# An adaLN attention and Mish MLP block on one core: the transposes of the last two blocks' normalised tiles go by 32 x 32 squares through DRAM and VectorE, and sums of weights are made at other places

## The chip, the cores and the metric

The kernel runs on one core of one Trainium2 chip. The metric is the device time in microseconds (us) of one execution. TensorE (PE) multiplies matrices out of SBUF into PSUM, VectorE (DVE), ScalarE (ACT) and GpSimd (POOL) work element by element, and SyncE (SP) and GpSimd issue most of the DMAs.

## The reference

2048 rows of 512 numbers; the MLP is 1792 wide. Everything is float32.

```
mod = (silu(c) @ w_mod).reshape(1, 6, 1, 512)
sa, ca, ga, sb, cb, gb = mod[:, 0..5]
h = layernorm(x) * (1 + ca) + sa
q, k, v = heads(h @ wqkv)                      # 32 heads of 16
phi = lambda t: where(t > 0, t + 1, exp(t)) + 1e-6
kv = einsum("bhsd,bhse->bhde", phi(k), v);  z = phi(k).sum over rows
o = einsum(phi(q), kv) / (einsum(phi(q), z) + 1e-6)
x = x + ga * (o @ wo)
h = layernorm(x) * (1 + cb) + sb
out = x + gb * (mish(h @ w1 + b1) @ w2)        # mish(t) = t * tanh(softplus(t))
```

## The kernel before

**Arithmetic.** Each operand of a matrix product is split into a high part `h` (rounded to the matmul's fp32r type, made on ScalarE or GpSimd) and a low part `l` (the rest, made on VectorE, L88 or L90). A product is three matmuls: high by high, low by high, high by low (`mm3`, lines L74 to L76 of the profile). q and the MLP use a scheme of seven products in place of eight on 2 x 2 blocks, for which sums and differences of the operands are made first: `q_left`/`q_right` for q, `rows` for w1, `columns` for the activations' side, `w2_sums` for w2, `left_sums` for its left operands.

**Blocks.** The rows are four blocks of 512, each of four tiles of 128 rows (`t`). A tile of x is normalised (`ln_side`: statistics, `ln_apply`), and the normalised tiles are needed in two layouts: as they are (`xn`, for `g_unit`, which sums k-by-x products) and turned (`hT`, for k and q). The turned tiles are made by `transpose`: sixteen 128 x 128 transposes on TensorE a block (L237) into a PSUM tile, from which ScalarE makes the scaled tile `hf` (L243), whose high and low parts are `hT`. After attention, the second normalisation makes n tiles (`norm_tile`); those of blocks 2 and 3 are stored to DRAM (`nd`), loaded back (`load_back`), and turned on TensorE by `transpose_f` (L919).

**Stages, by the profile's time.** Up to 24 us block 0 starts up; to 107 us `k_unit` and `g_unit` of blocks 1, 2, 3 alternate and end with z (the sum of phi(k), L295); to 130 us q of blocks 0 and 1 (`q_sevens`) and `kv_ps`, the product that gives kv (L968); to 157 us q of blocks 2 and 3, with m = kv by wo (`m_ps`) between; to 211 us the outputs `o_unit` and the second normalisation of blocks 0 and 1; to 312 us the MLP of these two (pairs of w1's tiles g, `pair_unit`, with `d_unit` for w2 behind); to 352 us the second half of that (`second`); to 436 us the pairs of blocks 2 and 3; to the end their sevenths with w2.

**What sets the order.** The code is in the order of execution for each engine. TensorE's work is written out; work for the other engines is in generators that are put on a list by `spawn`, and `tick()` moves each of these one step further (up to its next `yield`). A second list (`spawn_idle`) lets its first two (three in the last phase) move at each tick. So the place of a VectorE, ScalarE or DMA instruction is set by the tick in which its step falls, and an engine carries its instructions out in that order, waiting at each until its inputs are there. All tiles of 128 x 512 share one pool of 101 places.

**Weights.** `rows(g)` loads the two w1 tiles of pair g (L716), makes four sums and differences of 128 x 256 (L722 to L725) and splits them into high and low; `store_rows` writes the parts to DRAM for g below 5, and `load_rows` reads them back through GpSimd's queue (L756) for blocks 2 and 3. `w2_job(f)` scales a w2 tile by gb, splits it and stores the parts; for pairs below 5 it stores the scaled tile too (`w2f`). `w2_sums(g)` loads these (L671) or takes the tile at hand, makes four differences of 128 x 256 and splits them, and stores the result to `w2t`. `wo_scale` scales wo by ga and splits it. `z_side` makes what the denominator needs from z.

Of the kernel before, what the change touches and what calls it, by code (L numbers as in the profile page):

```python
# [13 lines left out]
P = 128  # L14
# [11 lines left out]
def block_kernel(ctx: ExitStack, tc: tile.TileContext, x, wqkv, wo, w1, b1t, w2, c, wmodt, out):  # L26
# [205 lines left out]

    def transpose(key, b, j, sc0, sh0, ptag, hi_engine=act):

        p = ps(ptag, f"tp_{key}_{b}_{j}")
        for t in range(4):
            pe.transpose(p[:, P * t:P * (t + 1)], xt[key, b, t][:, P * j:P * (j + 1)], ident)  # L237

        def post():
            hf = sb(f"hf_{key}_{b}_{j}")  # L240
            if b < 2:
                hfx[b, j] = hf
            act.activation(hf, p, AF.Identity, bias=mc[:, sh0 + j:sh0 + j + 1], scale=mc[:, sc0 + j:sc0 + j + 1])  # L243
            yield from split(f"hT_{key}_{b}_{j}", hf, hT, (key, b, j), hi_engine=hi_engine)
# [178 lines left out]
    def ln_side(b):  # L423
        for j in range(4):
            ln_stats("x", b, j, xt["x", b, j])
            if j == 3:
                ln_eps("x", b)
                ln_rstd("x", b)
            yield
        ln_shift("x", b)  # L430
# [165 lines left out]
    def wo_scale():  # L596

        for k in range(4):
            dve.tensor_tensor(wos[k], wos[k], bc["ga"], op=ALU.mult)
            yield  # L600
            yield from split(f"wos_{k}", wos[k], wos, k)
# [6 lines left out]
    def z_side():  # L608
# [7 lines left out]
        for g in range(4):  # L616
# [3 lines left out]
            dve.tensor_scalar(hmask[:, g, :], hmask[:, g, :], zc[:, g:g + 1], 1.0, op0=ALU.mult, op1=ALU.mult)  # L620
        for k in range(4):
            zs[k] = sb(f"zs_{k}")
            dve.tensor_scalar(zs[k], zbc, mc[:, k:k + 1], 1.0, op0=ALU.mult, op1=ALU.mult)

        dve.tensor_reduce(zh, zbc.rearrange("p (h r) -> p h r", r=16), op=ALU.add, axis=mybir.AxisListType.X)
# [17 lines left out]
    def w2_job(f, wait=2):  # L643
# [10 lines left out]
        if n == 0:  # L654
            w2f[g] = drp.tile([P, 2, D], F32, name=f"w2f_{g}")
# [4 lines left out]
        if g < KEPT:  # L660
            pool.dma_start(w2f[g][:, n, :], t)

    w2t, w2k, wb = {}, {}, {}
    W2_AT = {0: 6, 1: 5, 2: 0, 3: 1, 6: 2}

    def w2_sums(g):

        if g < KEPT:
# [26 lines left out]
        for i in range(2):  # L695
            for n in range(2):
                sp.dma_start(d[:, n, 2 * i:2 * i + 2, :], f32(keep[i][n]).rearrange("p (t c) -> p t c", t=2))
# [13 lines left out]
    def rows(g, wait):  # L711

        r = [sb(f"w1p_{g}_{i}", F32, (P, 4, P)) for i in range(2)]
        for i in range(2):
            f = 2 * g + i
            sp.dma_start(r[i], w1[:, P * f:P * (f + 1)].rearrange("(k p) f -> p k f", p=P))  # L716
        for _ in range(wait):
# [10 lines left out]
        op_rows[g] = keep  # L728
# [13 lines left out]
    op_rows, rows_d = {}, {}  # L742

    def store_rows(g):
# [684 lines left out]
```

## Time and profile before

| | us |
|---|---|
| median of 3 runs (lowest, highest) | 495.04 (493.94, 495.09) |
| span of the profiled execution | 493.7 |
| TensorE busy in it | 486.8 (99%) |
| VectorE busy | 370.3 (75%) |
| ScalarE busy | 298.1 (60%) |
| GpSimd busy | 144.0 (29%) |

The profiled execution's own time is its span and what lies around it; the times of the runs lie about 1.3 us above the span (495.04 to 493.7). A row of the profile names a line of the kernel, an engine, an operation and the tiles written and read, with buffer numbers left out. An engine that is idle has a releaser, the event that ended its wait.

### The profile page before, as it was taken

To read this page: it belongs to the slowest core of one execution; us is meant where nothing else is said; L and a number is where in the kernel's file an instruction comes from. 1 tells how busy PE (TensorE), PEld (TensorE's weight loads), DVE (VectorE), ACT (ScalarE), POOL (GpSimd) and SP (SyncE) were. 2 spreads that over 40 slices of the span, in tenths; PEclk is the share of its full clock that TensorE was granted. 3 is DMA by queue.
4 is the path that set the end of the run, shared out by engine and by line. 5 is a ranking of instruction groups with operands and counts; after the bars stand their busy time and mean duration, and the time that the engine had idled before them with its cause. 6 is when DMAs were issued, how large, how long until landed. Compare 5 with 4: busy or idle time off the path is not lost.

```text
span 493.7 us, 7708 instructions
## 1 busy us (share of the span) xinstructions
PE 486.8 (99%) x2638; PEld 412.0 (83%) x2638; DVE 370.3 (75%) x715; ACT 298.1 (60%) x533; POOL 144.0 (29%) x242
## 2 busy tenths in 40 slices
PE   7999999999999999999999999999999999999997
PEld 5788888878878888888888888888888888899997
DVE  6888889899799699976877563789732666769872
ACT  6886587866555879737767655288045555568100
POOL 3673111000023124103432435114644410545200
PEclk9999999999999999999999999999999999999999
DMA  8813545144873417388899979999996704688512
GB/s 303 295 43 90 163 100 118 43 132 148 285 197 108 107 54 254 117 283 304 271 327 312 308 237 280 333 289 357 387 309 193 218 23 123 179 206 229 134 44 86
DMA packets 66785, 98.58 MB, mean 200 GB/s; under 512 B 7057, under 2 KB 31641, under 8 KB 66746
## 3 DMA queue, kind: packets, MB, share of 16 engines
q1 hardware_dynamic: 37896, 53.63, 32.7%
q0 software_dynamic: 28704, 44.19, 32.5%
q8 instruction: 21, 0.34, 0.3%
q10 hardware_dynamic: 146, 0.26, 0.1%
q14 instruction: 18, 0.15, 0.1%
HBM read 62.92 MB, written 33.03 MB: 194 GB/s over the span
## 4 chain that ended last, share of the span: by engine, by line
PE 97%; DMA 1%; ACT 1%; DVE 0%; SPq 0%; issue 0%; DVEq 0%; ACTq 0%
PE p_a L1064 19%; PE p_s L1064 8%; PE oacc L76 5%; PE oacc L75 5%; PE oacc L74 5%; PE m L76 5%; PE m L75 5%; PE m L74 5%; PE o L74 3%; PE gacc L75 3%; PE gacc L76 3%; PE o L76 3%; PE gacc L74 3%; PE o L75 3%; PE pq_a L345 3%; PE pk L76 2%
## 5 line engine op out<-in xcount | busy, mean ns | idle before, releaser
L199 POOL TENSOR_TENSOR rs_n<-rs_n,half 128x1 f32<-128x1 f32 x16 | 11.4, 710 | 63.3 <-DVE rs_n L194 36.6
L1069 DVE TENSOR_TENSOR cb<-p_s,u 128x512 f32<-128x512 f32 x28 | 19.2, 687 | 13.0 <-ACT u L1105 13.0
L1099 ACT ACTIVATE u<-p_a 128x512 f32<-128x512 f32 x12 | 7.2, 598 | 29.0 <-PE p_a L1064 29.0
L1074 ACT ACTIVATE u<-p_a 128x512 f32<-128x512 f32 x14 | 8.4, 598 | 25.5 <-PE p_a L1064 25.5
L1056 ACT ACTIVATE ub<-cb,b1c 128x512 f32<-128x512 f32 x28 | 20.0, 717 | 4.9 <-DVE cb L1069 4.7
L1327 POOL DMA_DIRECT2D wt_m<-w2t x20 | 14.0, 702 | 26.8 <-DVE cb L1069 14.7
L921 ACT ACTIVATE hf_n<-tp_n,mc 128x512 f32<-128x512 f32 x16 | 11.7, 767 | 12.8 <-PE tp_n L919 12.8
L1105 ACT ACTIVATE u<-p_a 128x512 f32<-128x512 f32 x14 | 8.3, 596 | 17.0 <-PE p_a L1064 13.8
L709 POOL DMA_DIRECT2D w2b<-w2d x20 | 10.6, 532 | 24.0 <-DMA w2t<-t_5h 4.6
L259 DVE SCALAR_TENSOR_TENSOR ku<-e_k,relu_k 128x512 f32<-128x512 f32 x16 | 11.0, 688 | 7.1 <-ACT relu_k L257 7.0
L1069 DVE TENSOR_TENSOR c<-p_a,u 128x512 f32<-128x512 f32 x14 | 9.6, 689 | 8.5 <-PE p_a L1064 6.5
L256 ACT ACTIVATE e_k<-pk 128x512 f32<-128x512 f32 x16 | 9.5, 596 | 9.5 <-PE pk L76 9.5
L821 POOL DMA_DIRECT2D rden_d<-rden x2 | 1.4, 718 | 45.9 <-DVE rden L819 45.9
L703 POOL DMA_DIRECT2D wb<-w2d x14 | 9.9, 710 | 14.9 <-PE p_a L1064 12.4
L199 POOL TENSOR_TENSOR rs_x<-rs_x,half 128x1 f32<-128x1 f32 (+1 forms) x10 | 7.4, 742 | 23.3 <-DVE rs_x L194 22.5
L1033 ACT ACTIVATE u<-p_a,b1c 128x512 f32<-128x512 f32 x14 | 9.6, 687 | 6.9 <-PE p_a L1064 6.9
L259 DVE SCALAR_TENSOR_TENSOR q<-e_q,relu_q 128x512 f32<-128x512 f32 x16 | 10.7, 686 | 3.1 <-ACT relu_q L257 3.1
L208 ACT ACTIVATE x<-x,nb_x,rs_x 128x512 f32<-128x512 f32 x13 | 10.0, 808 | 4.9 <-DVE nb_x L203 3.8
L268 POOL DMA_DIRECT2D ku<-ku x8 | 7.2, 899 | 18.8 <-DVE ku L259 18.8
L845 DVE TENSOR_TENSOR r<-o,r 128x512 f32<-128x512 f32 x16 | 10.8, 677 | 1.0 <-PE o L76 0.9
L833 DVE SCALAR_TENSOR_TENSOR q<-q,rd 128x512 f32<-128x512 f32 x16 | 10.4, 685 | 1.1 <-DMA rd<-rden_d 1.1
L190 DVE BATCH_NORM_STATS2 st_x<-x 128x6 f32<-128x512 f32 x13 | 8.9, 681 | 2.9 <-DMA x<-in_x_dram 2.9
(1573 smaller groups left out, 1974.5 us busy)
## 6 DMA issues: line engine op xcount, KB each, us to landing
wm<-in_wmodt_dram SPq DMA_DIRECT2D x24, 256.0 KB, 5.8
w2b<-w2d POOLq DMA_DIRECT2D x20, 256.0 KB, 6.4
wt_m<-w2t POOLq DMA_DIRECT2D x20, 256.0 KB, 4.2
r<-in_x_dram SPq DMA_DIRECT2D x16, 256.0 KB, 2.8
x<-in_x_dram SPq DMA_DIRECT2D x15, 256.0 KB, 4.6
w1p<-in_w_dram SPq DMA_DIRECT2D x14, 256.0 KB, 5.2
w2r<-in_w_dram SPq DMA_DIRECT2D x14, 256.0 KB, 5.3
wb<-w2d POOLq DMA_DIRECT2D x14, 256.0 KB, 5.0
```

Of the source, the lines that this page charges most:

```text
L74: pe.matmul(o, st[0], mv[0], start=start, stop=False)
L75: pe.matmul(o, st[0], mv[1], start=False, stop=False)
L76: pe.matmul(o, st[1], mv[0], start=False, stop=stop)
L199: pool.tensor_tensor(y, y, half[:, lo:hi], op=ALU.pow)
L259: dve.scalar_tensor_tensor(dst, e, 1.0, r, op0=ALU.min, op1=ALU.add)
L345: pe.matmul(p, l, r, start=onto is None and c == 0 and i == 0, stop=c == 1 and i == 2, skip_group_check=onto is not None)
L845: dve.tensor_tensor(r, p, r, op=ALU.add)
L921: act.activation(hf[b, j], p, AF.Identity, bias=mc[:, 12 + j:13 + j], scale=mc[:, 16 + j:17 + j])
L1056: act.activation(u, p, AF.Mish, bias=b1c[:, f:f + 1])
L1064: pe.matmul(p, st, mv, start=onto is None and c == 0 and i == 0, stop=c == 1 and i == 2, skip_group_check=onto is not None)
L1069: dve.tensor_tensor(out, p, u, op=ALU.add)
L1327: pool.dma_start(v, w2t[g][:, :, SUM[name], :])
```

## The change

1. `ln_side` for blocks 2 and 3 stores each normalised tile in squares (`store_squares`: 128 x 16 x 32 numbers in runs of 32) and loads four tiles back (`load_squares`), both on SyncE's queue. `turn` turns 32 x 32 squares on VectorE (L251) and `scale_turned` makes `hf` from that with a strided read in SBUF. The same is done with the n tiles of blocks 2 and 3; `nd` and `load_back` go. The 64 transposes on TensorE go.
2. Block 2's statistics come two a step and its four tiles are normalised in one step. Block 3's statistics come from sums on ScalarE (`act_sums`) and not from VectorE.
3. w1's parts are no longer stored and read back: `load_w1` loads the two tiles, and `rows(g)` runs again for pairs 0 to 4 of blocks 2 and 3.
4. `w2_sums` for pairs 0, 1 and 2 runs in `w2_job`, from the tiles at hand, beside the first MLP; pairs 5 and 6 stay in `second`. The `w2t` stores of the three go through GpSimd's queue. w2 and w1 tiles are loaded a pair earlier.
5. `wo_scale` runs beside q and not beside `g_unit` of block 3; `z_side` has more steps; the mod columns 8 to 11 move from block 2 to block 3, two a step; `q_right` starts later; `rows(0)` runs as one piece between the matmuls of `kv_ps` and kv.

The core of the diff:

```diff
+    def store_squares(key, b, t, v, eng=sp):
+        if (key, b) not in squares:
+            squares[key, b] = drp.tile([16, 32, 4, 4, 32], F32, name=f"sq_{key}_{b}")
+        d = squares[key, b]
+        eng.dma_start(bass.AP(tensor=d.tensor, offset=d.offset + 32 * t, ap=[[P, P], [32 * D, 16], [1, 32]]),
+                      v.rearrange("p (a c) -> p a c", c=32))
+    def load_squares(key, b, j, eng=sp):
+        d = squares[key, b]
+        v = turned[key, b, j] = sb(f"sq_{key}_{b}_{j}")
+        eng.dma_start(v, bass.AP(tensor=d.tensor, offset=d.offset + P * D * j, ap=[[D, P], [1, D]]))
+    def turn(key, b, j):
+        v = turned[key, b, j]
+        turned[key, b, j] = sb(f"tq_{key}_{b}_{j}")
+        dve.transpose(turned[key, b, j], v)
...
     def ln_side(b):
+        if b == 2:
+            for j in range(4):
+                ln_stats("x", b, j, xt["x", b, j])
...
+                if j % 2:
+                    yield
+            ln_shift("x", b)
+        else:
+            for n in range(4):
+                for j in (2 * n, 2 * n + 1):
+                    if j < 4:
+                        sums[j] = act_sums("x", b, j, xt["x", b, j])
...
         for j in range(4):
             t = xt["x", b, j]
             ln_apply("x", b, j, t, t, act if b > 2 or j < 2 else dve)
-            if j % 2:
+            store_squares("x", b, j, t)
+            if j == 3 or j % 2 and b > 2:
                 yield
+        for j in range(4):
+            load_squares("x", b, j)
...
-        if g < KEPT:
+        if g in SUMS_KEPT:
             pool.dma_start(w2f[g][:, n, :], t)
+        elif g < KEPT and n:
+            yield
+            yield from w2_sums(g)
-    W2_AT = {0: 6, 1: 5, 2: 0, 3: 1, 6: 2}
+    W2_AT = {0: 6, 2: 5}
...
+    run(early_rows[0])
     for j in range(2):
         js = slice(64 * j, 64 * (j + 1))
         dve.tensor_tensor(kv.rearrange("p (g m) -> p g m", g=4)[js, :, js],
...
     for n, g in enumerate(pairs):
         if n < 5:
-            if n:
-                load_rows(n)
+            spawn_idle(rows(n, 0))
+            if n < 4:
+                load_w1(n + 1)
```

Three places in the order. First SyncE beside block 1's `k_unit`s (x_0 to x_3 in the loads are the tiles of block 3, those in the stores the tiles of block 2, sq_x the squares, wr a tile of wqkv). Before:

```order
25 L99 DMA x_0_532<-in_x_dram 128x512
26 L99 DMA x_1_558<-in_x_dram 128x512
27 L99 DMA x_2_591<-in_x_dram 128x512
28 L99 DMA x_3_624<-in_x_dram 128x512
29 L107 DMA wr_0_785<-in_wqkv_dram 128x512
```

Now:

```order
27 L240 DMA sq_x_544<-x_1_433 128x16x32
28 L240 DMA sq_x_544<-x_2_435 128x16x32
29 L240 DMA sq_x_544<-x_3_437 128x16x32
30 L99 DMA x_1_573<-in_x_dram 128x512
31 L246 DMA sq_x_0_575<-sq_x_544 128x512
32 L246 DMA sq_x_1_577<-sq_x_544 128x512
33 L246 DMA sq_x_2_579<-sq_x_544 128x512
34 L246 DMA sq_x_3_581<-sq_x_544 128x512
35 L99 DMA x_2_609<-in_x_dram 128x512
36 L99 DMA x_3_639<-in_x_dram 128x512
```

The stores and the read-back of block 2 stand ahead of the loads of two tiles of block 3. At block 1's `g_unit`s, ScalarE had pk_3h right between the scalings of block 2 (hf) and their high parts (hT); now it has (scrap and sums are block 3's statistics):

```order
62 L82 ACTIVATE pk_3h<-ku_3_648 128x512
63 L220 ACTIVATE scrap_x_0_677,sums_x_0_678<-x_0_540 128x512
64 L221 ACTIVATE scrap_x_0_677,sums_x_0_678<-x_0_540,sums_x_0_678 128x512
65 L220 ACTIVATE scrap_x_1_681,sums_x_1_682<-x_1_573 128x512
66 L221 ACTIVATE scrap_x_1_681,sums_x_1_682<-x_1_573,sums_x_1_682 128x512
67 L220 ACTIVATE scrap_x_2_703,sums_x_2_704<-x_2_609 128x512
68 L221 ACTIVATE scrap_x_2_703,sums_x_2_704<-x_2_609,sums_x_2_704 128x512
69 L220 ACTIVATE scrap_x_3_709,sums_x_3_710<-x_3_639 128x512
70 L221 ACTIVATE scrap_x_3_709,sums_x_3_710<-x_3_639,sums_x_3_710 128x512
71 L255 ACTIVATE hf_x_0_715<-tq_x_0_685,mc 128x512
72 L82 ACTIVATE hT_x_0h<-hf_x_0_715 128x512
```

Block 3's sums stand ahead of block 2's scalings. VectorE there (pk_3 is the fourth k tile of block 1, tq_x a turned tile):

```order
81 L291 SCALAR_TENSOR_TENSOR ku_3_648<-e_k_3_649,relu_k_3_650 128x512
82 L88 TENSOR_TENSOR xn_3l<-x_3_109,xn_3h 128x512
83 L251 STREAM_TRANSPOSE tq_x_0_685<-sq_x_0_575 128x512
84 L251 STREAM_TRANSPOSE tq_x_1_687<-sq_x_1_577 128x512
85 L90 SCALAR_TENSOR_TENSOR pk_3l<-ku_3_648,pk_3h 128x512
```

The two turns stand ahead of pk_3l. Second, VectorE ahead of kv, before (cq are q's sums, q phi of them):

```order
208 L259 SCALAR_TENSOR_TENSOR q_2_1452<-e_q_2_1464,relu_q_2_1465 128x512
209 L259 SCALAR_TENSOR_TENSOR q_3_1459<-e_q_3_1468,relu_q_3_1469 128x512
210 L356 TENSOR_TENSOR cq_0_1510<-pq_s_0_1476,qu_0_1383 128x512
211 L356 TENSOR_TENSOR cq_1_1519<-pq_s_1_1486,qu_1_1408 128x512
212 L971 TENSOR_TENSOR kv<-kv_ps,bmask 64x4x64 x2
```

and now (w1p are w1's tiles, s their sums, a_0l and s_0l low parts):

```order
208 L388 TENSOR_TENSOR cq_1_1510<-pq_s_1_1473,qu_1_1383 128x512
209 L88 TENSOR_TENSOR wos_3l<-wo_1047,wos_3h 128x512
210 L790 TENSOR_TENSOR s_0_1580<-w1p_1_1140 128x256
211 L791 TENSOR_TENSOR s_0_1580<-s_0_1580,w1p_0_1139 128x256
212 L792 TENSOR_TENSOR s_0_1581<-w1p_0_1139,w1p_1_1140 128x256
213 L793 TENSOR_TENSOR s_0_1581<-w1p_0_1139,s_0_1580 128x256
214 L88 TENSOR_TENSOR a_0l<-w1p_0_1139,a_0h 128x512
215 L88 TENSOR_TENSOR s_0l<-s_0_1580,s_0h 128x512
216 L88 TENSOR_TENSOR s_0l<-s_0_1581,s_0h 128x512
217 L88 TENSOR_TENSOR a_0l<-w1p_1_1140,a_0h 128x256
218 L1024 TENSOR_TENSOR kv<-kv_ps,bmask 64x4x64 x2
```

Eight operations on w1 and one on wo stand between the last q sums and kv. Third, VectorE beside the `o_unit`s of block 3 (w2r are scaled w2 tiles, t_0_2446 and t_0_2447 their differences, r the residual):

```order
343 L893 TENSOR_TENSOR r_0_1631<-o_0_2399,r_0_1631 128x512
344 L742 TENSOR_TENSOR t_0_2446<-w2r_2076 128x256
345 L742 TENSOR_TENSOR t_0_2446<-w2r_2078,t_0_2446 128x256
346 L742 TENSOR_TENSOR t_0_2447<-w2r_2078,w2r_2076 128x256
347 L742 TENSOR_TENSOR t_0_2447<-t_0_2446,w2r_2078 128x256
348 L88 TENSOR_TENSOR b_1_1l<-hf_n_1_2397,b_1_1h 128x512
349 L982 TENSOR_TENSOR t_1_0_2464<-hf_n_1_2397,hf_n_1_2277 128x512
```

The four differences of w2's pair 0 (L742) were made in `second` before, and are now ahead of the differences of the activations (L982).

More of the change, by code (lines that the diff above doesn't have):

```diff
@@ L596, in wo_scale @@
     def wo_scale():
[L598 to L599 removed]
+        halves = []
+        for k in range(6):
+            if k > 1:
+                next(halves[k - 2], None)
+            if 0 < k < 5:
+                halves.append(split(f"wos_{k - 1}", wos[k - 1], wos, k - 1))
+                next(halves[-1])
+            if k < 4:
+                dve.tensor_tensor(wos[k], wos[k], bc["ga"], op=ALU.mult)
             yield
[L601 removed]
     zc = cst.tile([P, 4], F32, name="zc")
@@ L709, in w2_again, with load_w1 @@
             pool.dma_start(w2s[f][i], w2d[f // 2, i][:, f % 2, :])
-    def rows(g, wait):
-        r = [sb(f"w1p_{g}_{i}", F32, (P, 4, P)) for i in range(2)]
+    w1r = {}
+    def load_w1(g):
+        r = w1r[g] = [sb(f"w1p_{g}_{i}", F32, (P, 4, P)) for i in range(2)]
         for i in range(2):
@@ L716, in rows @@
             sp.dma_start(r[i], w1[:, P * f:P * (f + 1)].rearrange("(k p) f -> p k f", p=P))
+    def rows(g, wait):
+        if g not in w1r:
+            load_w1(g)
+        r = w1r.pop(g)
         for _ in range(wait):
```

117 lines of the change are left out of this document (63 added, 54 removed).

## The prediction

> **What bounds the kernel now.** I read the page first: the busy shares and the chain that ended last.
>
> ```profile
> span 493.7 us, 7708 instructions
> PE 486.8 (99%) x2638; PEld 412.0 (83%) x2638; DVE 370.3 (75%) x715; ACT 298.1 (60%) x533; POOL 144.0 (29%) x242
> PE 97%; DMA 1%; ACT 1%; DVE 0%; SPq 0%; issue 0%; DVEq 0%; ACTq 0%
> ```
>
> TensorE is busy for 486.8 of 493.7 us and is 97% of the chain. The view of waits, for TensorE, then lists in five rows what it ever waited for, 1.1 us at most; the last of them in the program:
>
> ```profile
> PE gacc L75 <- DVE pk_0l L90: 0.2, 1, 0.2
> ```
>
> All five lie in the first 25 us. From then on TensorE never waits, so each microsecond taken off it is a microsecond gained, unless a wait appears that was not there. The question is therefore twofold: how much TensorE work goes, and which of its inputs, now that TensorE is earlier, come too late. For the second the busy times by stage matter (start:end, length, then PE, PEld, DVE, ACT, POOL; DMA share and GB/s last):
>
> ```profile
> 44.00:60.00 16.00, 16.00 (x80) 13.42 (x79) 14.42 (x26) 12.28 (x21) 2.64 (x3) 1.00 0.62 148
> 91.00:123.00 32.00, 32.00 (x144) 25.34 (x143) 31.56 (x68) 22.38 (x43) 0.74 (x2) 1.00 0.41 121
> 130.40:159.60 29.20, 29.20 (x183) 23.45 (x184) 29.05 (x62) 14.60 (x29) 7.32 (x12) 1.00 0.62 173
> 188.20:214.80 26.60, 26.60 (x126) 22.01 (x125) 26.46 (x44) 19.42 (x34) 6.34 (x12) 1.00 0.55 179
> 313.00:340.00 27.00, 27.00 (x137) 22.69 (x136) 22.02 (x45) 18.03 (x32) 6.09 (x12) 1.00 0.94 310
> 340.00:352.00 12.00, 11.99 (x53) 9.47 (x52) 11.96 (x21) 5.53 (x11) 8.40 (x15) 1.00 1.19 373
> 352.00:375.00 23.00, 23.00 (x114) 19.47 (x113) 7.03 (x12) 10.55 (x17) 11.90 (x22) 1.00 0.97 281
> 375.00:400.00 25.00, 25.00 (x134) 21.62 (x133) 13.47 (x22) 12.84 (x21) 8.57 (x15) 1.00 0.70 197
> ```
>
> VectorE has no room in 91 to 123, 130 to 160, 188 to 215 and 340 to 352 us (31.56 of 32, 29.05 of 29.2, 26.46 of 26.6, 11.96 of 12): whatever is put there delays all behind it. It has plenty in 352 to 400.
>
> **What goes from TensorE.** 64 transposes: four groups of 8 of x tiles (blocks 2 and 3) and four of n tiles. In the chain, where overlap is taken out, the first and the last of these eight groups (start, us, count) are
>
> ```profile
> 48.19 0.87 PE tp_x L237 x8
> 332.56 0.87 PE tp_n L919 x8
> ```
>
> so 8 x 0.87 = 6.98 us go: 1.75 us before 58 us, 3.5 by 85 us, the rest between 313 and 333. No other matmul goes. This is the ceiling of the gain: 493.7 - 7.0 = 486.7 in the span.
>
> **The way round through DRAM (blocks 2 and 3 of x).** A tile is now stored in 2048 pieces of 128 bytes, 128 to each DMA engine, read back as four 256 KB tiles, turned on VectorE (two turns ahead of pk_3l), scaled on ScalarE. The trace has no piece of 128 bytes. Its nearest rows are a lone store of 128 pieces of 512 bytes (with 4 tiny ones) over 2 us, and loads of 2 KB pieces over 3.5 us (queue: packets, MB, share of 16 engines); SyncE's rows give the delay round a store that is read back.
>
> ```profile
> q1 hardware_dynamic: 132, 0.07, 11.8%
> q1 hardware_dynamic: 689, 1.25, 98.5%
> 161.23 0.68 SPq L821 DMA_DIRECT2D rden_d<-rden  x1
> 163.80 0.63 SPq L825 DMA_DIRECT2D rd<-rden_d  x1
> ```
>
> 0.118 x 2.0 x 16 / 132 is 29 ns a piece of 512 bytes; 0.985 x 3.5 x 16 / 689 is 80 ns on average with 80 small pieces in it, some 87 ns for 2 KB. The line through 29 and 87 has a start of 10 ns and gives **13 ns at 128 bytes**; the other end is **29 ns**, that a short piece costs as much as one of 512. I take 13, since it follows the line of both rows, and keep 29 for a rival. A square store is then 128 x 13 = 1.7 us, four of them 6.7; the read-back of the store above began 2.6 us after its issue, of which 1 us were packets, so 1.6 us is added. Block 2 is normalised after rows of this kind; behind them, what TensorE needs next, the landing of a 256 KB load, and what ScalarE is given between (L220 and its accumulator are half of one tile's sums, L221 the other half):
>
> ```profile
> 36.36 1.07 POOL L84 CAST hT_x_3h<-hf_x 128x512 fp32r<-128x512 f32 x1
> 36.88 1.09 DVE L88 TENSOR_TENSOR hT_x_2l<-hf_x,hT_x_2h 128x512 fp32r<-128x512 f32 x1
> 40.48 1.02 POOL L199 TENSOR_TENSOR rs_x<-rs_x,half 128x4 f32<-128x4 f32 x1 [3.05 <-DVE rs_x L194]
> 44.28 1.52 ACT L208 ACTIVATE x<-x,nb_x,rs_x 128x512 f32<-128x512 f32 x2
> 58.24 0.39 PE L75 MATMUL gacc<-pk_3l,xn_3h 128*128 128x512 f32 x1
> 60.73 0.39 PE L74 MATMUL pk<-wk_0h,hT_x_0h 128*128 128x512 f32 x1
> 64.77 0.69 DVE L259 SCALAR_TENSOR_TENSOR ku<-e_k,relu_k 128x512 f32<-128x512 f32 x1 [2.09 <-ACT relu_k L257]
> 81.80 0.39 PE L75 MATMUL gacc<-pk_3l,xn_3h 128*128 128x512 f32 x1
> 103.58 1.06 PE L295 MATMUL z<-ku,ones 128*32 128x512 f32 x8
> L724 DVE TENSOR_TENSOR s<-w1p,w1p 128x256 f32<-128x256 f32 x7 | 2.9, 417 | 0.0
> r<-in_x_dram SPq DMA_DIRECT2D x16, 256.0 KB, 2.8
> L220 ACT ACTIVATE scrap_x<-x 128x512 f32<-128x512 f32 x3 | 1.9, 640 | 0.0
> L221 ACT ACTIVATE scrap_x<-x,sums_x 128x512 f32<-128x512 f32 x3 | 2.2, 723 | 0.1
> L220 ACT ACTIVATION_READ_ACCUMULATOR scrap_n<-r 128x1 f32 x10 | 1.9, 187 | 0.0
> 80.43 0.76 ACT L243 ACTIVATE hf_x<-tp_x,mc 128x512 f32<-128x512 f32 x1
> 81.22 0.63 ACT L82 ACTIVATE hT_x_2h<-hf_x 128x512 fp32r<-128x512 f32 x1
> ```
>
> All four statistics now come in one go, so the power on GpSimd moves from 40.5 to about 37.5 (the end of its last cast), and the four tiles are normalised from 39 to 41; the first store leaves at about 40.2. Packets from 40.8, landed 40.8 + 6.7 + 1.6 = 49.1, first two tiles back at 49.1 + 2.8 = 51.9, turned by 53.2, pk_3l by 53.9. TensorE needs pk_3l at 58.24 - 1.75 = 56.5: 2.6 us to spare, so **no stall here at 13 ns**, and the limit is 13 + 2.6/0.51 = 18 ns. (Each ns on a piece costs 512 pieces per engine, 0.51 us.)
>
> But the SyncE order puts x tiles 2 and 3 of block 3 behind the read-back, which waits until the stores have landed: those two issue at about 51 and, sharing the engines with four read-backs, land near 54 and 55. ScalarE must make their sums (1.5 us a tile: 0.64 + 0.72 + 2 x 0.19, less overlap) **ahead of** block 2's four scalings: the sums end at 57, and four pairs of scaling and high part (0.76 + 0.63, 1.35 from start to start) end at 62.4, the last low part at 63.1. TensorE needs that low part 11 matmuls of 0.227 us behind 60.73 - 1.75, at 61.5: **1.6 us late**. Towards z, VectorE then has 58 operations of 512 columns (0.60 from start to start) and 8 of 256 (0.42 long, 0.36 from start to start), 37.7 us; before, it began them at 64.8, now at 63.0 + 1.6, and ends at 102.3, while TensorE wants the last at 104.3 - 3.5 = 100.8 (the z row: its fourth quarter): 1.5, the same delay over again and not a second one; with some idle time in the stretch I write **1.8 us up to z**, bounds 0 (GpSimd's and ScalarE's order overlapping better) and 3.
>
> What a turn takes is in no row. Bounds: 0.60 as every other 512-column operation of VectorE here from start to start, and 1.10, the slowest such row (hT_x_2l above, beside a GpSimd cast); I take 0.60, to which most rows are near. At 1.10 the eight turns of x would add at most 4 us and the eight of n at most 4.
>
> **kv.** Rows(0), eight VectorE operations, now stand ahead of kv.
>
> ```profile
> 127.31 0.69 DVE L356 TENSOR_TENSOR cq<-pq_s,qu 128x512 f32<-128x512 f32 x1 [0.22 <-PE pq_s L345]
> 128.22 2.08 PE L968 MATMUL kv_ps<-zs,wv 128*64 128x64 f32 x64
> 137.29 0.68 DVE L88 TENSOR_TENSOR kvl<-kv,kvh 128x512 fp32r<-128x512 f32 x1
> 138.99 0.39 PE L76 MATMUL m_ps<-wos_0h,kvl 128*128 128x512 f32 x1
> ```
>
> Before, VectorE was idle from 128.0 to 130.35, kv_ps's end. Now wos_3l (0.6), four sums (4 x 0.37) and the low parts (3 x 0.60 + 0.36) fill 128.0 to 132.2: kv comes 1.9 late. VectorE is full from there on, so kvl is as late; it had 138.99 - 137.97 = 1.0 to spare: **0.9 us** (0.7 to 1.1).
>
> **w2's sums beside the first MLP.** Those of pair 0 now fall ahead of the t_1l that the first p_s reads.
>
> ```profile
> 210.05 1.28 DVE L88 TENSOR_TENSOR t_1l<-t,t_1h 128x512 fp32r<-128x512 f32 x2
> 212.26 0.39 PE L1064 MATMUL p_s<-t_1l,s_0h 128*128 128x512 f32 x1
> ```
>
> Four of 256 columns (1.5) and two low parts (1.2) make 2.7 us on a full VectorE; the first t_1l ended at 210.73, 1.5 before it was read: **1.2 us** (0 to 1.5, if the low parts fall behind it).
>
> **313 to 352.** VectorE loses three pairs' sums, 3 x 2.7 = 8.1, and gets eight turns, 4.8; TensorE arrives 3.5 earlier. 0.2, from 0 to 0.5: **0.25 us**. The GpSimd loads of w1's parts (8 a pair) and the stores of them go, so the DMA engines, at a share of 1.19 from 340 to 352, get room. GpSimd takes over twelve w2t stores from SyncE and gives up forty loads; busy for 6.09 of 27 us, it holds nobody up: nothing.
>
> **352 to 436.** Per pair, w1's sums and low parts bring VectorE 4 x 0.36 + 3 x 0.6 + 0.36 = 3.6 us and ScalarE 3.5 halves, 2 us. Five pairs bring 18 us, into stretches where VectorE was idle for 16 of 23 and 11.5 of 25: nothing. If that cover failed, a pair would cost what it exceeds it by, at most 1 us.
>
> The rest (z's steps apart, mod columns moved one block, wo scaled beside q) moves work between neighbours of the same full stretch, and is inside the bounds of the first two terms.
>
> **Sum.** 6.98 - 1.8 - 0.9 - 1.2 - 0.25 = 2.8 us of gain. From the profiled execution's span, 493.7, that is 490.9; the times shown (median 495.04) lie 1.3 above that span, so the forecast is **492.2**.
>
> **Rivals.** *All of it hidden.* The orders on VectorE and ScalarE keep ahead, and TensorE again never waits: 495.04 - 6.98 = 488.1. For it: stalls of 1 to 2 us at four places are small against my reading of them (starts are known to some 0.5 us). Against it: VectorE's three full stretches.
>
> *Dear pieces: slower than before.* If a 128-byte piece written to DRAM costs what one of 512 does, 29 ns, four stores take 14.8 us, block 2's first tiles are back at 40.8 + 14.8 + 1.6 + 2.8 = 60.0 and pk_3l is there at 62.0 instead of 56.5: 5.5 late. Block 3's stores start near 63, when its first two tiles are normalised, and their way takes 14.8 + 4.4 + 2 just the same, to 84, against 81.8 - 3.5 = 78.3 at which g needs its pk_3l (read in the trace at 81.80): another 5.5, less what the first delay has moved. With 9 in place of 1.8 the time is 495.0 - 7.0 + 9 + 2.35 = 499.4. It decides from 18 ns on; at 23 the gain is gone. [...] No run here shows a write that small; what the rows show is 29 ns at 512.
>
> *No change worth the name.* Turns at 1.10 us (4 us on the full stretches before z, of which the idle time in them takes 1 to 2), or 20 to 23 ns a piece: 2 to 4 us more, 494 to 496.5. [...]
>
> **How the numbers follow.** A measurement of this kernel can tell 0.3%, 1.5 us, from no change: the bounds are 493.55 and 496.5. The forecast's case (490 to 493.5) 0.42, all hidden (488 to 490) 0.2, no change 0.15, dear pieces 0.23. So faster 0.62, same 0.15, slower 0.23. Leaving out the lowest tenth and the upper half of the dear case gives 488.5 to 499.0.
>
> **What would show it.** Right: in the profile after, TensorE's chain has no tp_x of blocks 2 and 3; square stores take about 1.7 us of packets; waits of TensorE on hT_x low parts near 61, on kvl near 136, on t_1l near 208, 1 to 2 us each. Wrong: waits for pk_3l ended by a DMA of sq tiles (dear pieces), no waits at all (hidden), or turns over 0.8 us. A wait between 352 and 436 would break the cover that I rely on.

## The result and the profile after

The changed kernel takes 508.12 us (median of 4 runs, 507.03 to 509.34), the kernel before 494.82: a ratio of 1.0272, 95% interval 1.0254 to 1.029. The forecast was 492.2 with a range up to 499.0: the change makes the kernel 13.3 us slower, not 2.6 faster. The page's lines, as shown of before:

```profile
span 506.2 us, 7500 instructions
PE 488.2 (96%) x2574; PEld 406.3 (80%) x2574; DVE 393.7 (78%) x769; ACT 321.5 (64%) x569; POOL 120.6 (24%) x203
PE 70%; DVE 13%; ACT 9%; DMA 4%; issue 2%; POOL 1%; SPq 0%; DVEq 0%; ACTq 0%
```

TensorE was 97% of the chain and is 70%. The 64 transposes are gone (2574 matmuls for 2638), yet its busy time did not fall by 7 us but rose by 1.4. The view of waits for TensorE, those behind 25 us of 0.6 us or more:

```profile
PE gacc L75 <- DVE pk_3l L90: 2.8, 1, 2.8
PE gacc L75 <- DVE rs_x L225: 2.7, 1, 2.7
PE pk L74 <- ACT hT_x_0h L82: 1.2, 1, 1.2
PE m_ps L76 <- DVE kvl L88: 0.9, 1, 0.9
PE p_s L1119 <- DVE t_1l L88: 0.9, 1, 0.9
PE p_a L1119 <- ACT u L1160: 0.7, 1, 0.7
PE pk L74 <- ACT hT_x_1h L82: 0.6, 1, 0.6
PE gacc L75 <- DVE pk_2l L90: 0.6, 1, 0.6
```

Both long waits are for pk_3l: the matmul that reads it waits, once in block 1's g and once in block 2's (at block 1's the view names rs_x, the VectorE instruction next to it). Where the time went is seen by the start of the same matmul in the two profiled executions:

```
matmul                                    before    after   difference
gacc <- pk_2h (block 1, third tile)        55.17    52.67     -2.50
gacc <- pk_3l (block 1)                    58.24    58.47     +0.23
pk <- wk_0h (block 2)                      60.73    64.03     +3.30
pk <- wk_3h, hT_x_3l (block 2)             63.23    70.35     +7.12
gacc <- pk_3l (block 2)                    81.80    90.28     +8.48
pk <- wk_3h, hT_x_3l (block 3)             86.79    97.30    +10.51
zbc <- zsum                               107.44   120.37    +12.93
kv_ps <- zs                               128.22   141.46    +13.24
m_ps <- kvl                               138.99   153.33    +14.34
p_s <- t_1h (the matmul ahead of t_1l)    212.03   226.54    +14.51
p_s <- t_1l                               212.26   227.79    +15.53
oacc <- a_8l                              347.59   359.39    +11.81
p_s <- s_5l                               367.46   380.13    +12.68
```

15.4 us are lost between 52.7 and 120 us, in a stretch from which 1.7 us of transposes went, so 17.1 in all; 1.1 between kv_ps and m_ps, 1.0 at w2's first sums; 3.7 come back where the n tiles are no longer turned on TensorE; 0.9 go at the start of the last pairs. So the question is what took 17.1 us at the x tiles, where 1.8 was forecast.

The chain there, first for block 2, then block 3's turn (start, us):

```profile
54.26 4.84 DMA x<-in_x_dram
59.89 0.81 ACT scrap_x L221 x2
60.70 0.62 ACT scrap_x L220 x2
61.34 0.81 ACT scrap_x L221 x2
62.16 1.17 ACT hf_x L255
68.94 0.63 ACT hT_x_3h L82
83.29 5.63 DMA sq_x<-sq_x
89.58 0.66 DVE pk_3l L90
```

A load of block 3 lands at 59.1, its sums on ScalarE end at 62.1, and only then come block 2's four scalings. The rows of SyncE's queue say why that load is late:

```profile
39.17 7.19 SPq L240 DMA_DIRECT2D sq_x<-x  x4
46.41 3.69 SPq L99 DMA_DIRECT2D x<-in_x_dram  x1
51.66 2.56 SPq L246 DMA_DIRECT2D sq_x<-sq_x  x4
54.26 0.91 SPq L99 DMA_DIRECT2D x<-in_x_dram  x2
```

Issuing four square stores held SyncE for 7.2 us and the next load for another 3.7, where an issue mostly takes 0.33 to 0.42 us before. The stores had landed at 51.7, the other two x loads went out at 54.3. The queues from 39 to 50 us:

```profile
q1 hardware_dynamic: 7764, 0.99, 59.5%
q0 software_dynamic: 288, 0.52, 27.8%
```

A piece of 128 bytes takes 0.595 x 11 x 16 / 7764 = 13.5 ns, as forecast. But beside them run the accumulating copies of k's features (ku), 288 packets in 0.278 x 11 x 16 = 49 us, 170 ns each, twice what a 2 KB packet of a load took before (80 to 87). VectorE's turns and ScalarE's scalings, as rows:

```profile
55.91 0.71 DVE L251 STREAM_TRANSPOSE tq_x<-sq_x 128x512 f32<-128x512 f32 x1 [6.06 <-DMA sq_x<-sq_x]
57.13 0.71 DVE L251 STREAM_TRANSPOSE tq_x<-sq_x 128x512 f32<-128x512 f32 x1 [0.51 <-DMA sq_x<-sq_x]
57.76 0.65 DVE L90 SCALAR_TENSOR_TENSOR pk_3l<-ku,pk_3h 128x512 fp32r<-128x512 f32 x1
L255 ACT ACTIVATE hf_x<-tq_x,mc 128x512 f32<-128x512 f32 x8 | 10.4, 1297 | 2.8 <-DVE tq_x L251 2.8
```

VectorE stood 6 us in front of a turn with pk_3l behind it; a scaling with strided reads takes 1.30 us, where the one from PSUM took 0.77. And behind its long waits TensorE is slow; busy times by stretch, the granted clock in the third column from the end:

```profile
55.00:58.00 3.00, 0.78 (x4) 0.32 (x2) 1.58 (x3) 0.52 (x2) 0.00 (x0) 1.00 1.03 333
60.00:62.50 2.50, 2.50 (x7) 1.75 (x6) 0.44 (x4) 2.47 (x7) 0.63 (x2) 0.50 0.00 0
67.00:69.00 2.00, 1.75 (x5) 0.79 (x3) 0.69 (x1) 1.94 (x4) 0.00 (x0) 0.50 0.00 0
88.00:90.20 2.20, 0.00 (x0) 0.00 (x0) 1.61 (x4) 1.78 (x2) 0.00 (x0) 0.93 1.05 380
90.20:93.00 2.80, 2.72 (x6) 2.15 (x7) 2.80 (x6) 2.77 (x5) 0.00 (x0) 0.50 1.06 401
```

From 60 to 62.5 and from 90.2 to 93 TensorE is all but fully busy with 7 and 6 matmuls: the clock is 0.50, a step 0.427 us and not 0.227. The clock is also 0.50 around 68 us, and there no single wait was long: those ahead of it, on hT_x_0h and hT_x_1h, are 1.2 and 0.6 us. The waits between 53 and 121 us add up to 8.8 us (those above and short ones). The other 8.3 of the 17.1 us are matmul steps that are longer without a listed wait: some 5 at half clock, an estimate from these three stretches, the rest mostly steps of 0.3 to 0.4 us next to the waits.

### The profile page after: what moved, and what is told of

Its sections match the earlier page's. It is cut to its first block, busy times and chain, and to the rows that moved or that the text cites. A ratio compares the mean times of both kernels' runs of the same rounds, so it can differ in the third digit from the quotient of the medians.

```text
span 506.2 us, 7500 instructions
## 1 busy us (share of the span) xinstructions
PE 488.2 (96%) x2574; PEld 406.3 (80%) x2574; DVE 393.7 (78%) x769; ACT 321.5 (64%) x569; POOL 120.6 (24%) x203
## 4 chain that ended last, share of the span: by engine, by line
PE 70%; DVE 13%; ACT 9%; DMA 4%; issue 2%; POOL 1%; SPq 0%; DVEq 0%; ACTq 0%
PE p_a L1119 18%; PE p_s L1119 7%; PE oacc L76 5%; PE oacc L75 5%; PE oacc L74 5%; PE m L76 5%; PE m L75 5%; PE m L74 5%; PE o L74 3%; PE o L76 3%; PE o L75 3%; ACT hf_x L255 2%; DMA x<-in_x_dram 2%; DMA sq_x<-x 2%; DVE wm L175 1%
## 5 line engine op out<-in xcount | busy, mean ns | idle before, releaser
L199 POOL TENSOR_TENSOR rs_n<-rs_n,half 128x1 f32<-128x1 f32 x16 | 9.8, 610 | 59.3 <-DVE rs_n L225 46.5
L255 ACT ACTIVATE hf_n<-tq_n,mc 128x512 f32<-128x512 f32 x8 | 10.3, 1336 | 8.3 <-DVE tq_n L251 7.5
L199 POOL TENSOR_TENSOR rs_x<-rs_x,half 128x1 f32<-128x1 f32 (+1 forms) x13 | 9.0, 695 | 21.3 <-DVE rs_x L194 10.1
L251 DVE STREAM_TRANSPOSE tq_x<-sq_x 128x512 f32<-128x512 f32 x8 | 5.4, 699 | 10.7 <-DMA sq_x<-sq_x 10.7
L75 PE MATMUL gacc<-pk_3l,xn_3h 128*128 128x512 f32 x16 | 7.9, 491 | 5.5 <-DVE pk_3l L90 2.8
L255 ACT ACTIVATE hf_x<-tq_x,mc 128x512 f32<-128x512 f32 x8 | 10.4, 1297 | 2.8 <-DVE tq_x L251 2.8
```

Of the source, the lines that this page charges most:

```text
L75: pe.matmul(o, st[0], mv[1], start=False, stop=False)
L199: pool.tensor_tensor(y, y, half[:, lo:hi], op=ALU.pow)
L255: act.activation(dst.rearrange("p (t i f) -> p t i f", t=4, f=4), turned.pop((key, b, j)).rearrange("p (f t i) -> p t i f", f=4, t=4), AF. ...
```

## The experiments

Times are medians; each ratio is to the kernel before, run on the same chip. The kernel before had medians of 494.62 to 495.08 there, so a difference of half a microsecond between two runs of different chips says nothing.

| run | us | ratio, 95% interval |
|---|---|---|
| the change | 508.12 | 1.0272 (1.0254 to 1.029) |
| x_on_pe | 495.80 | 1.0025 (1.0013 to 1.0038) |
| x_early | 501.90 | 1.0147 (1.0132 to 1.0162) |
| flat_scale | 505.19 | 1.0217 (1.0200 to 1.0234) |
| whole_rows | 499.68 | 1.0103 (1.0088 to 1.0118) |
| pieces_512 | 502.57 | 1.0164 (1.0147 to 1.0181) |
| no_accum | 504.72 | 1.0206 (1.0190 to 1.0222) |
| all_four | 499.75 | 1.0100 (1.0085 to 1.0115) |
| three | 494.69 | 0.9996 (0.9986 to 1.0006) |
| x_early_stats | 501.73 | 1.0137 (1.0119 to 1.0155) |
| three_stats | 493.65 | 0.9978 (0.9968 to 0.9988) |
| x_on_pe_kv | 498.00 | 1.0061 (1.0040 to 1.0081) |
| n_only | 495.00 | 1.0009 (0.9999 to 1.0019) |
| n_only_w2late | 491.08 | 0.9923 (0.9906 to 0.9940) |
| wait_gap4 | 494.70 | 0.9994 (0.9985 to 1.0003) |
| wait_start5 | 495.23 | 1.0006 (0.9996 to 1.0015) |
| hold_u3 | 503.69 | 1.0176 (1.0158 to 1.0193) |
| hold_u2 | 499.31 | 1.0080 (1.0049 to 1.0110) |

**x_on_pe.** The x tiles' way alone is undone:

```diff
-        if b < 2:
+        if True:
             p = ps(ptag, f"tp_{key}_{b}_{j}")
...
-            store_squares("x", b, j, t)
-        for j in range(4):
-            load_squares("x", b, j)
-            if not last and t:
-                for tr in turning:
...
+            if not last and t % 2 == 0:
+                for j in (t, t + 1):
+                    tr = transpose("x", b + 1, j, 4, 0, "tp" if j == t else "h")
```

> The x tiles of blocks 2 and 3 are turned on TensorE again, in the order of the kernel before; their square stores, read-backs and turns go. All else of the change stays (block 3's sums on ScalarE, n tiles by squares, w1 and w2 sums moved). Theory A, the way of the x tiles through DRAM and VectorE costs the 15 us that TensorE lost between 53 and 107 us: 494 to 497 us, no wait of TensorE on pk_3l. Theory B, the moved statistics, mod columns and wo scaling overload ScalarE and VectorE there, whoever turns the tiles: above 502 us.

495.8 us: theory A. The x tiles' way through DRAM costs 12.3 us net, and since it takes 3.5 us of transposes off TensorE, some 15.8 in all. Block 3's sums on ScalarE and the other moved work bring no wait on pk_3l. The rest of the change, with 3.5 us less of transposes, is still 0.25% slower than before.

**x_early.** SyncE's order is changed:

```diff
-            if b + 2 < NB:
-                load_x(b + 2, t)
+            if b + 2 < NB and t == 0:
+                for j in range(4):
+                    load_x(b + 2, j)
```

> The changed kernel with all four x loads of block 3 issued ahead of block 2's square stores on SyncE's queue. Theory A1, the loads held up behind stores and read-back delay block 3's sums on ScalarE and so block 2's scalings: the sums end 6 us earlier, hT of block 2 comes 4 to 6 us earlier, 502 to 504 us. Theory A2, the turned tiles themselves come too late (DMA engines full of small pieces): ScalarE waits for the turns instead, 506 to 508 us. Theory A3, the scalings are too slow: 505 to 507.

501.9 us, 6.2 less: the loads held up behind the stores (A1) were in block 2's path. The wait on pk_3l stays.

**flat_scale.** The scaling reads in order (this leaves the reordering out):

```diff
-        act.activation(dst.rearrange("p (t i f) -> p t i f", t=4, f=4),
-                       turned.pop((key, b, j)).rearrange("p (f t i) -> p t i f", f=4, t=4), AF.Identity,
+        act.activation(dst, turned.pop((key, b, j)), AF.Identity,
```

> The changed kernel with the scalings of turned tiles reading SBUF in order and not with strides; the reordering of columns is left out, so the products use columns of other rows. A scaling falls from 1.29 us to about 0.75. Theory A3, the slow scalings are on the path of both blocks: 4 x 0.55 less for each of blocks 2 and 3, and less slow clock behind the waits, 502 to 504 us. Theory A1 or A2, ScalarE mostly waits for sums or turns: one or two scalings count, 506 to 507 us.

505.2, 2.9 less, between the two theories. The group of scalings there:

```profile
L255 ACT ACTIVATE hf_x<-tq_x,mc 128x512 f32<-128x512 f32 x8 | 6.4, 806 | 2.5 <-DVE tq_x L251 2.5
```

0.81 us for 1.30: the strides cost 0.49 a tile, 3.9 for eight, and 2.9 of that came through.

**whole_rows** (leaves the squares out) and **pieces_512** (likewise):

```diff
-        eng.dma_start(bass.AP(tensor=d.tensor, offset=d.offset + 32 * t, ap=[[P, P], [32 * D, 16], [1, 32]]),
-                      v.rearrange("p (a c) -> p a c", c=32))
+        eng.dma_start(bass.AP(tensor=d.tensor, offset=d.offset + P * D * t, ap=[[D, P], [1, D]]), v)
```

```diff
+        eng.dma_start(bass.AP(tensor=d.tensor, offset=d.offset + P * t, ap=[[D, P], [P * D, 4], [1, P]]),
+                      v.rearrange("p (a c) -> p a c", c=P))
```

> The changed kernel with the tiles of x and n stored in whole rows of 2 KB and not in pieces of 128 bytes (16 times fewer pieces); the squares are left out, so the turned tiles hold other numbers. Four stores take 2.8 us of the engines' time and not 6.9. Theory A2, the pieces fill the DMA engines and hold SyncE's queue: read-back 4 us earlier in both blocks, no wait on pk_3l, 498 to 502 us. Theory A1 or A3: the sums and scalings stay late, 504 to 507 us.

> The changed kernel with square stores in pieces of 512 bytes, four times fewer, each read-back still needing all four stores (the squares are left out, so the turned tiles hold other numbers). Whole rows also let each read-back start after one store. If the pieces themselves cost (13 ns a 128-byte piece, 27 a 512-byte one: 6.9 us of the engines against 3.5 for four stores, and SyncE is not held): 501 to 503 us, a wait on pk_3l of 0 to 1 us. If the dependence on all four stores is what costs: 506 to 508 us.

499.7 and 502.6 us, 8.4 and 5.5 less; in both no wait on pk_3l is left. SyncE's rows with pieces of 512 bytes:

```profile
38.81 2.31 SPq L240 DMA_DIRECT2D sq_x<-x  x4
41.18 0.86 SPq L99 DMA_DIRECT2D x<-in_x_dram  x1
44.34 2.44 SPq L246 DMA_DIRECT2D sq_x<-sq_x  x4
46.82 0.99 SPq L99 DMA_DIRECT2D x<-in_x_dram  x2
```

The four issues take 2.3 us and not 7.2, the read-back starts at 44.3 and not 51.7. The profiled execution of pieces_512 is its fastest (500.04 us; the other three took 502.3 to 503.7), so for those it is not shown that no such wait is left. That each read-back needs all four stores can account for no more than about the 2.9 us between the two medians.

**no_accum.** `pool.dma_start(ku[0, t], ..., accum_op=ALU.add)` becomes `pool.tensor_tensor(ku[0, t], ku[0, t], ku.pop((b, t)), op=ALU.add)`.

> The changed kernel with the eight additions of k's features (ku of blocks 1 and 2 onto block 0's) made on GpSimd out of SBUF and not by accumulating DMAs, whose 2 KB packets took about 190 ns each beside the square stores. Theory A2b, these copies take the engines' time that the stores needed: read-back some 4 us earlier in both blocks, 501 to 503 us. Rival, the stores are slow by themselves (SyncE's queue, the way to DRAM): 506 to 509, GpSimd's adds slowing VectorE a little.

504.7, less of a gain than forecast. SyncE's rows:

```profile
38.69 5.13 SPq L240 DMA_DIRECT2D sq_x<-x  x4
47.47 2.13 SPq L246 DMA_DIRECT2D sq_x<-sq_x  x4
```

The four issues take 5.1 us and not 7.2, and the read-back goes out at 47.5 and not 51.7. The first wait on pk_3l is gone, the second falls to 1.1. In their place stand waits on the high parts of hT (1.7 us on hT_x_0h, and in two waits each 1.6 on hT_x_2h and 1.2 on hT_x_3h), which ScalarE makes behind its late and slow scalings, and a slower VectorE, seen in the next run.

**all_four, then three** (the same without the GpSimd additions; both leave squares and reordering out).

> The four edits at once on the changed kernel: early x loads, scalings that read in order (reordering left out), stores in whole rows (squares left out), additions on GpSimd. If the four costs together are what the way of the x tiles costs: no wait over 0.5 us between 53 and 107 us, 491 to 494 us. If something else there costs too (VectorE's order, sums on ScalarE): 495 to 498 us.

> The changed kernel with early x loads, scalings in order (reordering left out) and stores in whole rows (squares left out), but the additions of k's features by accumulating DMAs as in the change. All four edits together were no faster than whole rows alone, and there VectorE's operations beside a GpSimd addition took 1.6 to 1.8 us and not 0.69. Theory C1, that slowing gave back what the other edits won: 495 to 497 us. Theory C2, GpSimd's adds cost nothing that counts, and the limit is block 3's sums on ScalarE ahead of block 2's scalings: 499 to 500 us as with all four.

499.75 with all four, no better than whole rows alone: the expectation was missed. Without GpSimd's additions 494.7, a little below the range of theory C1. Rows of all_four, a GpSimd addition and the VectorE instruction beside it:

```profile
66.43 1.61 POOL L298 TENSOR_TENSOR ku<-ku,ku 128x512 f32<-128x512 f32 x1 [7.94 <-DVE ku L289]
66.80 1.80 DVE L357 TENSOR_TENSOR qt<-hf_x,hf_x 128x512 f32<-128x512 f32 x1
```

The same instruction of VectorE takes 0.68 us in the run called three. Seven VectorE instructions between 43 and 80 us took 1.60 to 1.80 us there, each beside such an addition; over the whole run VectorE is busy for 401.2 us in all_four and 393.3 in three, so the eight additions cost it about 8 us. So the accumulating copies do take the DMA engines' time, and the other way is dearer. With the three edits 13.4 us come back, as much as the change had cost net (13.3), though by themselves they gave 6.2, 2.9 and 8.4: they share delays. Of the 15.8 us of the x tiles' way, 2.4 are still there. The long waits of TensorE that are left in three:

```profile
PE p_s L1118 <- DVE t_1l L88: 1.2, 1, 1.2
PE warm L136 <- POOL ones L130: 1.1, 1, 1.1
PE m_ps L76 <- DVE kvl L88: 0.9, 1, 0.9
```

**x_early_stats and three_stats.** Block 3's statistics go to VectorE (`if b == 2:` in `ln_side` becomes `if True:`).

> The changed kernel with early x loads, and block 3's statistics on VectorE, two a step, as block 2's, so that ScalarE has no sums ahead of block 2's scalings. Nothing is left out. Theory D1, the sums' place on ScalarE costs block 2 some 4 us once the turned tiles are there: 497 to 499.5 us (501.9 with early loads alone). Theory D2, the turned tiles are what is late, and VectorE's statistics stand ahead of the turns: 501 to 503 us.

> Early x loads, scalings in order, whole rows (reordering and squares left out), and block 3's statistics on VectorE. If late loads, small pieces, strided scalings and the sums' place on ScalarE are all that the x tiles' way costs, no wait over 0.5 us between 53 and 107 us is left and the time is that of the kernel with x on TensorE less the 3.5 us of its transposes: 492 to 493.5 us. If something else costs there, 494 to 497 us.

501.7 against 501.9, theory D2: while the turned tiles are late, the sums' place on ScalarE is worth nothing. Once they are not late it is worth 1.0 us (493.65 against 494.69), and no wait over 0.5 us is left between 53 and 107 us. It is still 1.3 us above x_on_pe less its 3.5 us of transposes; some 0.7 of this is in its waits (0.5 on pk_2l, and 0.4 on t_1l where x_on_pe has 0.2), the rest was not settled.

**x_on_pe_kv.** `run(early_rows[0])` ahead of kv goes, and `spawn_idle(early_rows[0])` stands behind kv.

> The changed kernel with x turned on TensorE (495.8 us), and rows(0) no longer ahead of kv on VectorE but in the idle queue behind it. If rows(0) makes kvl late, the 0.9 us wait of m_ps for kvl goes and the time is 494.8 us; if wo's scaling beside q does, it stays at 495.8.

498.0, slower by 2.2: neither expectation. The wait on kvl is gone, so rows(0) was its cause, but a new one stands in its place:

```profile
PE o L76 <- DVE qs_2l L88: 2.0, 1, 2.0
```

The eight operations are now in the next full stretch, ahead of qs_2l, and behind that wait TensorE ran at a clock of 0.50 from 157 to 160 us.

**n_only and n_only_w2late.** From the kernel before: the n tiles alone go by squares; then also the sums of w2's pairs 0 to 2 move into the last pairs.

```diff
-        d = nd[b, t] = drp.tile([P, D], F32, name=f"nd_{b}_{t}")
-        pool.dma_start(d, v)
+        yield
+        yield
+        store_squares("n", b, t, v)
...
-                transpose_f(*order.pop(0), "h")
+                spawn(turn_f(*order.pop(0)))
```

```diff
-    W2_AT = {0: 6, 1: 5, 2: 0, 3: 1, 6: 2}
+    W2_AT = {0: 6, 2: 5}
...
+        if n in (0, 1, 2):
+            spawn_idle(w2_sums(n))
         if n in (3, 5):
```

> The kernel before with the n tiles of blocks 2 and 3 alone going by squares (stored beside the first MLP, read back at its end, turned in the second half); x, w1 and w2 stay as before. Theory N1, a way with 10 us and more of time to spare costs nothing and the 3.5 us of TensorE come through, less what VectorE, full from 340 to 352 us, cannot take: 4.8 us of turns there are late by 2 to 4 us: 493 to 495 us. Theory N2, the turns find room: 491.3 us.

> The same, and the sums of w2's pairs 0, 1 and 2 (8 us of VectorE) moved from the second half of the first MLP into the pairs of blocks 2 and 3, where VectorE was idle for two thirds of the time. By the sum of the parts, 494.8 - 3.5 = 491.3 us, with no wait of TensorE behind 313 us; if the late loads of these pairs' tiles are missed at 436 us, 492 to 494.

495.0, the dear end of N1, no change: the two long waits in its trace,

```profile
PE oacc L76 <- DVE a_6l L88: 1.4, 1, 1.4
PE oacc L76 <- DVE a_7l L88: 0.8, 1, 0.8
```

are VectorE's full stretch at 340 us. With w2's sums in the last pairs 491.1, **faster than both kernels**, by 0.8% of before; no wait of TensorE above 0.5 us is left after 25 us. Its stretches:

```profile
340.00:352.00 12.00, 12.00 (x54) 9.93 (x54) 6.72 (x12) 0.77 (x2) 6.53 (x12) 1.00 1.20 329
352.00:375.00 23.00, 23.00 (x115) 19.47 (x114) 12.50 (x23) 13.21 (x22) 7.29 (x14) 1.00 0.83 265
```

VectorE has 6.72 of 12 us where it had 11.96, and 12.50 of 23 where it had 7.03: the work lies where there was room.

**What a wait costs.** Four kernels from before, in a stage with room on all engines. First `load_rows(3)` is moved from `n == 3` to a place two thirds through pair 4 (wait_gap4) and to the start of pair 5 (wait_start5):

> The kernel before with one set of w1 parts (pair 3, eight loads on GpSimd's queue) loaded two thirds through the pair ahead of its use and not two pairs ahead, in a stage where no other engine is full: TensorE gets one wait for a DMA of some 1 to 4 us. Theory K1, a wait of TensorE costs its length: the time rises by the wait that the trace shows, within 0.3 us. Theory K2, behind a wait of 2.5 us and more TensorE runs at half clock for 3 to 4 us, as it seemed at 60 and 91 us of the changed kernel: the time rises by the wait and 1.5 to 2 us more.

> The same with these loads at the start of the pair that uses them: a wait of 5 us or more, then shorter ones for the later parts. K1: the time rises by the waits of the trace. K2: by the waits and about 2 us for each stretch of half clock, read as matmul steps of 0.43 us where 0.227 is usual.

No wait arose and no change of the time: GpSimd's queue was ahead of TensorE, and the loads were in time (in wait_start5 they were issued from 402.5 to 408.3 us; in the kernel before TensorE reads the first of these tiles at 412.0). Then the loads were held back by data (hold_u3; hold_u2 has (0, 3) and the earlier tile u2):

```diff
+                if (c, m) == (1, 3):
+                    d = drp.tile([P, D], F32, name="hold_d")
+                    sp.dma_start(d, last_u["u3"])
+                    pool.dma_start(sb("hold"), d)
+                    load_rows(3)
```

> The two kernels with a late load brought no wait, since GpSimd's queue runs ahead of TensorE. Here the same eight loads of w1's parts are held on that queue behind a tile that goes to DRAM and back and that ScalarE makes from the pair before, past its middle. Their data land 7 to 11 us behind that, TensorE reaches them after 6: a wait of 1 to 4 us, then perhaps shorter ones. K1, a wait costs its length: the time rises by the waits shown. K2, behind a wait of 2.5 us and more TensorE runs at half clock for 3 to 4 us: the waits and 1.5 to 2 us more, with matmul steps of 0.43 us in the trace.

> The same, held behind an earlier tile, some 4 us before: a wait below 1 us or none. K1 and K2: the time rises by no more than the wait, and no step of 0.43 us is seen.

The waits in the trace of hold_u3 and of hold_u2, the stretches around the first and the one behind the second (clock third from the end):

```profile
PE p_a L1065 <- DMA a1b<-rd_a: 5.7, 1, 5.7
```

```profile
PE p_a L1065 <- DMA a1b<-rd_a: 2.2, 1, 2.2
```

```profile
405.00:411.00 6.00, 6.00 (x39) 5.37 (x38) 3.95 (x7) 4.99 (x9) 0.14 (x1) 1.00 0.24 81
417.50:422.70 5.20, 5.20 (x12) 4.06 (x13) 0.00 (x0) 1.21 (x2) 1.46 (x3) 0.50 1.16 312
423.00:428.00 5.00, 5.00 (x29) 4.37 (x28) 2.36 (x4) 1.84 (x3) 0.00 (x0) 1.00 0.00 0
```

```profile
414.80:417.80 3.00, 3.00 (x8) 2.30 (x7) 0.00 (x0) 1.21 (x2) 0.34 (x1) 0.50 1.19 365
```

A wait of 5.7 us costs 8.9 (503.69 less 494.81), one of 2.2 costs 4.5: K2, with 11 steps of 0.43 us in the one and 7 in the other. For the short wait the expectation of below 1 us was missed, and half clock came with it all the same. Its price is less firm than the long one's: the four executions of hold_u2 lie between 497.06 and 499.75, and only the profiled one (499.03, 4.2 above before) has a trace. The slow steps add up to 4.7 us behind the long wait and 3.0 behind the short one, at a granted clock of 0.50 in both stretches. A lone wait of 0.9 us (kvl in the change) brought no such steps (clock 1.00 from 153 to 157 us, steps of 0.23 us), but short waits close together did: whole_rows has waits of 0.60, 0.64 and 0.64 us that end at 60.1, 62.0 and 63.9 us, and behind them this stretch:

```profile
64.80:68.00 3.20, 3.20 (x8) 2.51 (x8) 2.59 (x5) 3.10 (x6) 0.57 (x1) 0.50 0.71 243
```

So in these runs the length of a single wait did not decide it; what does was not measured.

## Why the prediction was wrong, point by point

**The ceiling, 6.98 us, was right in kind.** The second half, 3.5 us for n, came through: the difference falls from 15.5 to 11.8 where n was turned, and the term of 0.25 us for 313 to 352 was nothing. **The first, 3.5 us for x, was swallowed.**

**"No stall here at 13 ns" and "1.8 us up to z" failed: 17.1 us.** The price of a piece, on which I hung the rival, was right (13.5 ns), with some luck: the line through 29 and 87 ns gives 14.5 at 128 bytes, and not the 13 that I read from it. Either is below the limit of 18. What was missing, in the order of the chain:

- *The pieces' time was taken for the stores' time.* I had the engines free for them. The accumulating copies ran beside them; the stores had landed at 51.7, not 49.1, and no_accum brought the read-back to 47.5.
- *The queue was taken to be free while the stores ran.* I let the other x loads wait for the landing, but 128-byte pieces held SyncE itself, 7.2 us for four issues and 3.7 for the load behind them (pieces_512: 2.3 and 0.9; no_accum, without the copies beside them: 5.1 and 2.3). The read-back that I let land 2.8 us after its issue shared the engines with the loads behind it (DMA share 1.03 from 55 to 58 us): first tiles turned at 56.6 and 57.8, not 53.2. That ended my 2.6 us to spare.
- *The order on ScalarE was read right, its times were not.* Sums end at 57 in the sum, 62.1 in the trace, since their tiles landed at 59.1 and not at 54 to 55 (x_early).
- *A scaling from SBUF was priced as one from PSUM*, 0.76 us; with the strides it is 1.30 (flat_scale). hT's last low part came at 70.3 and not at 63.1. In the run called all_four, where early loads, pieces and scalings are as I assumed, ScalarE's sums stand ahead and that low part runs from 63.2 to 63.9: the chain itself was drawn right.
- *A wait was priced at its length.* With the half clock behind it, a long one costs 2 to 3 us more (hold_u3, hold_u2); here some 5 us in all, by the trace, one of the three stretches behind short waits.
- *Block 3 was given no wait of its own.* The same stores and copies delayed its squares: VectorE waited for them and pk_3l came 2.8 us late.

**Rows(0) ahead of kv, 0.9 us: right**, 0.9 in the waits, 1.1 with TensorE's offset. x_on_pe_kv shows that it is rows(0), and that the one other place tried costs more.

**w2's sums, 1.2 us: right here**, 0.9 in the view of waits, 1.0 in the offset. No run moves the sums alone, and in runs that keep them the wait on t_1l is anywhere from 0.2 (x_on_pe) to 1.2 us (three): the size hangs on the rest of the order too.

**352 to 436, "nothing": off by 0.7.** I looked at VectorE alone. The wait of p_a is for ScalarE, where high parts of w1 now stand ahead of u.

**"The rest is inside the bounds": off by about 1 us**, z and zbc, where TensorE waits 0.4 us for ga_row, which moved one block later. It stays in x_on_pe, as do the waits on kvl (0.9) and on u (0.7).

**The dear-pieces rival** had the right place, the right sign and the wrong reason; its threshold of 18 ns was drawn with a free queue and free engines. Which share each of queue, copies and strides has cannot be given as a sum, since alone they give 17.5 us and together 13.4. That the three have most of it is shown (three: 13.4 of 15.8 us, and 1.0 more with block 3's statistics on VectorE); that the half clock has some 5 us of the loss is read from the trace of the change, not measured by itself there.

## What to carry to other kernels

In this kernel the detour through DRAM cost what its queue and its engines were doing at that time, not its bytes: the kernel took 8.4 us less with the same bytes in whole rows, and 6.2 less with block 3's loads ahead of the stores (whole_rows, x_early). So read, for the stretch in question, what else is on them, who stands behind each issue, and who stands behind the instruction that waits for the data. Where the detour had time to spare (the n tiles of the change were read back from 304.5 us on and turned from 328.9 on) it cost nothing that the runs show, and the gain then depended on VectorE, which took the work over, having room in that stage, or being given it (n_only: 495.00 us; n_only_w2late, with room made: 491.08, 3.5 less than before on the same chip, as much as the transposes of n took). A wait of TensorE of 2.2 us cost here 2.3 us above its length and one of 5.7 us 3.2, so price a wait by its length and the half clock behind it, and look for short waits in a row, which brought it here as well (whole_rows).

## What the runs showed of the hardware that was not expected

- Behind a wait of 2.2 us and of 5.7 us TensorE's matmul steps were 0.43 us and not 0.227, for 3 to 5 us, at a granted clock of 0.50 (hold_u2, hold_u3); behind a lone one of 0.9 us (kvl in the change) the clock was 1.00, but behind three of 0.6 us within 4 us it was 0.50, with 8 matmuls in 3.2 us (whole_rows).
- Issuing a store of an x tile in 2048 pieces held SyncE's queue for up to 3.6 us (median 0.67; four in a row took 7.2), one in 512 pieces for 0.6 on average (2.31 for four, pieces_512).
- Packets of an accumulating DMA took 169 to 197 ns for 2 KB (before, 42 to 50 us: 169; the change, 39 to 50: 170, and 71 to 83: 197). Those of a load took 80 on average with 80 small ones among 689 (before, 18.5 to 22 us), some 87 without these by my estimate from that row.
- ScalarE took 1.30 us for a 128 x 512 scaling with strided reads in SBUF, 0.81 in order (the change, flat_scale).
- VectorE's turn of 128 x 512 by 32 x 32 squares took 0.69 to 0.70 us (means of the eight of n and the eight of x in the change), most of its other operations of that size there 0.68 to 0.69.
- VectorE's operation took 1.80 us and not 0.68 beside a GpSimd addition of two SBUF tiles (1.61) in all_four; the 0.68 is from three.
